# Five small changes to an attention and feed-forward kernel: fewer products of zeros, two copies moved to VectorE, a buffer swapped, a product put later, the last output split

## The chip, the cores and the metric

One core of a Trainium2 chip. The metric is the device time of the whole program in microseconds (us), median of several runs on the same chip. The spread of one kernel's runs is mostly 1 to 2 us of 924 (3.7 us once), and the changes here are of that size. So experiments were timed in five rounds on one chip beside the kernel before (three chips in all, so a kernel is compared with its own runs of the kernel before), and each also left one profile in which stages can be compared to 0.1 us.

## The reference

Attention in which a query sees only the keys of its own hash bucket, then a two-layer product with a PReLU between.

```python
def _attn_ref(q, k, v, proj):            # q, k, v: (4, 8, 768, 64), proj: (64, 6)
    q_bits = (np.einsum('bhsd,dk->bhsk', q, proj) > 0)   # k_bits likewise, then bucket numbers
    mask = q_bucket[:, :, :, None] == k_bucket[:, :, None, :]
    scores = np.where(mask, scale * np.matmul(q, k.transpose(0, 1, 3, 2)), -1e9)
    attn = np.exp(scores - max); attn = attn / (sum + 1e-09)
    return np.matmul(attn, v)
def _moe_ref(x, w_in, w_out, alpha):     # x: (3072, 512), d_ff 2048
    h = x @ w_in
    g = np.maximum(h, 0.0) + alpha * np.minimum(h, 0.0)
    return (g @ w_out)
```

## The kernel before

Attention runs in 32 units (16 pairs of heads, two halves of the queries). A unit has six key tiles. For each, TensorE writes scores into one of three score buffers of two banks, ScalarE takes the exp into SBUF, and VectorE and an accumulating transfer issued by GpSimd add up the six tiles. `attend` multiplies the exps with v into the only bank `av`; `totals` multiplies the sum with ones into the only bank `sm`; `divide` (VectorE) reads both. VectorE also prepares the weights meanwhile. The feed-forward blocks are called f_0 to f_7 and z_1 to z_7 in the profile, four times over; their weights come by transfers `wi` and `wl`. Other names in the profile: `sc` scores, `pt` exps, `accd` and `accp` the two partial sums of the key tiles (the accumulating transfer adds into `accp`, VectorE's last sum adds `accp` to `accd`), `x` the divided result. A transfer "lands" when its data have arrived.

```python
    def setup():
        ...
        ps = psum.tile([P, 512], F32, name="nil", tag="av")
        for i in range(12):
            do(PE.matmul(ps, zero[:, :P], zero, start=True, stop=True))
    def setup_alpha():
        ps = psum.tile([P, NF], F32, name="alps", tag="sm")
        do(PE.transpose(ps, alpha16, ident[:NF, :NF]))
        do(DVE.tensor_copy(alpha, ps))
    def two_banks(name):
        return psum.tile([P, 2, 512], F32, name=name, tag="sc", bufs=3)
    ...
    for u in range(UNITS):
        scores(u, 1)
        if u < last:
            scores(u + 1, 0)
        add_last(u); add_total(u)              # VectorE: sum of six key tiles
        ...                                    # next unit's first sum, hash, turns, weights
        attend(u, 0)                           # key tiles 0 to 2
        totals(u)                              # ones product
        ...                                    # weights
        attend(u, 1)                           # key tiles 3 to 5
        divide(u)
        ...
    for j, (b, what, n) in enumerate(blocks):  # feed-forward
        ...
            load_w(b * NI + n + 2)             # wi, two buffers
            if n >= NI - 2:
                load_w2(b, n - NI + 2)         # wl
```

`do` keeps an engine's instructions in program order. Transfers without it are placed on their queue by the framework.

## Time and profile before

| | |
|---|---|
| time | 924.33 us median of 3; medians of 924.2 to 924.7 in the later comparisons |
| first profile | span 923.9 us; that run took 925.64 us |
| TensorE busy | 907.8 us |
| TensorE gaps | head 6.25, attention from 250 us on about 2.6, tail 7.1 us |

"Span" is the profile's own length, some 1.8 us less than the time. The first profile came from a run 1.3 us above the median. One more piece: the chain of waits where attention ends (start, length, what ran).

```profile
359.58 0.97 DVE accd L721
360.55 0.04 issue
360.59 0.87 PE sm L743 x4
361.46 1.94 PE av L731 x12
363.39 1.49 PE f_0a L805 x4
```

VectorE's last sum ends at 360.54, then come the ones product and three key tiles of attend, and feed-forward goes on at 363.39.

### The profile page before, as it was taken

The page shows a single profiled execution, that of the slowest core. Times are in us where ns is not written, and L with a number is a line of the kernel's source. Part 1 is how long each engine was busy: PE and PEld are TensorE (multiplying, and loading weights), DVE is VectorE, ACT ScalarE, POOL GpSimd, SP SyncE. Part 2 cuts the span into 40 slices and gives each one's busy share as a digit, 9 for nine tenths or more (in the row PEclk, how much of TensorE's full clock was granted, in tenths as well). Part 3 has the DMA queues.
Part 4 walks back from the last instruction along what each step waited for, and adds up shares of the span by engine and source line. Part 5 has one row for each costly group of instructions (what it writes and reads, how often), then busy time and mean ns, then how long its engine had stood idle before and what let it go on. Part 6 is the DMA issues. An engine that isn't in the chain of part 4 may idle for free.

```text
span 923.9 us, 13627 instructions
## 1 busy us (share of the span) xinstructions
PE 907.8 (98%) x5073; PEld 605.4 (66%) x5073; DVE 754.0 (82%) x1316; ACT 422.6 (46%) x751; POOL 40.9 (4%) x50
## 2 busy tenths in 40 slices
PE   7999999999999999999999999999999999999996
PEld 4444444454444444556998556998556998556996
DVE  3899998999999998678987668978668978668985
ACT  7788888888877783222212222212222212222212
POOL 1111111111111110000000000000000000000000
PEclk9999999999999999999999999999999999999999
DMA  9576969798777844425333325334325333321232
GB/s 240 145 188 158 273 162 301 177 254 240 189 188 190 205 131 148 174 92 186 110 134 131 116 101 180 109 131 140 112 105 177 111 133 138 112 105 40 100 131 70
DMA packets 114059, 141.50 MB, mean 153 GB/s; under 512 B 54064, under 2 KB 102208, under 8 KB 110400
## 3 DMA queue, kind: packets, MB, share of 16 engines
q1 hardware_dynamic: 103680, 127.56, 43.4%
q0 software_dynamic: 8704, 12.58, 8.0%
q8 instruction: 42, 0.69, 0.3%
q10 hardware_dynamic: 1600, 0.39, 0.2%
q14 instruction: 33, 0.27, 0.1%
HBM read 100.67 MB, written 27.26 MB: 138 GB/s over the span
## 4 chain that ended last, share of the span: by engine, by line
PE 65%; DVE 16%; DMA 2%; issue 1%; ACT 0%; DVEq 0%; ACTq 0%
PE sc L698 3%; PE z_4a L805 2%; PE f_4a L805 2%; PE z_7a L805 2%; PE z_5a L805 2%; PE z_3a L805 2%; PE z_6a L805 2%; PE z_2a L805 2%; PE z_1a L805 2%; PE f_2a L805 2%; PE f_5a L805 2%; PE f_7a L805 2%; PE f_6a L805 2%; PE f_1a L805 2%; PE av L731 2%; PE f_0a L805 2%
## 5 line engine op out<-in xcount | busy, mean ns | idle before, releaser
L703 ACT ACTIVATE pt<-sc 128x768 f32<-128x768 f32 x192 | 153.1, 814 | 61.8 <-PE sc L698 60.1
L698 PE MATMUL sc<-qT,kT 64*128 64x384 f32 x768 | 155.1, 482 | 0.0
L731 PE MATMUL av<-pt,vn 128*64 128x385 f32 (+1 forms) x768 | 136.5, 491 | 0.0
L731 PEld LDWEIGHTS av<-pt,vn 128*64 128x64 f32 x768 | 52.3, 136 | 70.7 <-issue 63.8
L698 PEld LDWEIGHTS sc<-qT,kT 64*128 64x128 f32 x768 | 68.1, 188 | 34.8 <-issue 34.7
L855 DVE TENSOR_TENSOR g<-g,g 128x384 f32<-128x384 f32 x128 | 68.4, 555 | 2.2
L698 PE MATMUL sc<-qb,kb 64*128 64x384 bf16 x384 | 63.0, 324 | 2.8 <-ACT kb L684 2.2
L895 DVE TENSOR_TENSOR ws<-wl 128x512 f32<-128x512 f32 x56 | 38.5, 688 | 24.0 <-DMA wl<-w_out_s 24.0
L903 DVE TENSOR_TENSOR gs<-g,gs 128x768 f32<-128x768 f32 x56 | 53.5, 956 | 1.0
L903 DVE TENSOR_TENSOR gs<-g 128x768 f32<-128x768 f32 x56 | 53.4, 953 | 0.0
L713 POOL DMA_DIRECT2D accp<-pt x32 | 38.5, 1204 | 311.4 <-DVE accp L712 150.2
L851 DVE SCALAR_TENSOR_TENSOR g<-h,alpha 128x384 f32<-128x384 f32 x32 | 19.8, 618 | 36.0 <-ACT h L844 36.0
L698 PEld LDWEIGHTS <-kb 64*128 64x128 bf16 x384 | 19.2, 94 | 43.2 <-issue 19.9
L712 DVE TENSOR_TENSOR accp<-pt,pt 128x768 f32<-128x768 f32 x32 | 30.4, 951 | 10.0 <-ACT pt L703 10.0
L679 ACT ACTIVATE qb<-hs,hb 32x384 bf16<-32x384 f32 x64 | 36.7, 574 | 2.2 <-issue 1.1
L721 DVE TENSOR_TENSOR accd<-accd,accp 128x768 f32<-128x768 f32 x32 | 30.7, 958 | 5.1 <-DMA accp<-pt 4.1
L717 DVE TENSOR_TENSOR accd<-pt,pt 128x768 f32<-128x768 f32 x32 | 30.5, 952 | 3.6 <-ACT pt L703 3.6
L718 DVE TENSOR_TENSOR accd<-accd,pt 128x768 f32<-128x768 f32 x32 | 30.7, 959 | 3.3
L915 DVE TENSOR_TENSOR m<-m,m 128x768 f32<-128x768 f32 (+1 forms) x40 | 28.6, 716 | 1.9 <-ACT m L921 1.2
L743 PE MATMUL sm<-accd,ones 128*64 128x384 f32 x128 | 26.5, 492 | 3.2 <-DVE accd L721 3.1
L684 ACT ACTIVATE kb<-hs,hb 64x384 bf16<-64x384 f32 (+1 forms) x48 | 27.7, 578 | 0.6
L564 DVE TENSOR_SCALAR_CACHE_REDUCE wx<-wx 128x512 f32<-128x512 f32 x32 | 21.7, 679 | 2.9 <-ACT wx L558 2.9
(323 smaller groups left out, 1777.7 us busy)
## 6 DMA issues: line engine op xcount, KB each, us to landing
wi<-w_in_s SPq DMA_DIRECT2D x32, 896.0 KB, 4.6
wl<-w_out_s SPq DMA_DIRECT2D x28, 1024.0 KB, 4.8
accp<-pt POOLq DMA_DIRECT2D x32, 384.0 KB, 4.3
raw<-in_moe_w_in_dram SPq DMA_DIRECT2D x16, 512.0 KB, 4.0
raw<-in_moe_w_out_dram SPq DMA_DIRECT2D x16, 512.0 KB, 3.8
w_in_s<-wsi SPq DMA_DIRECT2D x16, 448.0 KB, 5.4
w_out_s<-wso SPq DMA_DIRECT2D x8, 896.0 KB, 5.5
vn<-in_v_dram SPq DMA_DIRECT2D x16, 384.0 KB, 4.5
```

The costliest lines, as they stand in the source:

```text
L679: do(ACT.activation(bits["q", pi][D * s : D * s + 32, cols], ps[c : c + 32, half, :CW], AF.Sign, bias=hb[c : c + 32],))
L698: do(PE.matmul(sc[:, s, :CW], what["k", pi][r, ks], what["q", pi][r, qs], start=first, stop=not first,))
L703: do(ACT.activation(pt[:, :, :CW], sc[:, :, :CW], AF.Exp, scale=SCALE / DOWN))
L713: nc.gpsimd.dma_start(accp[u], p(u, 2), accum_op=ALU.add)
L717: do(DVE.tensor_tensor(accd[u], p(u, 3), p(u, 4), op=ALU.add))
L718: do(DVE.tensor_tensor(accd[u], accd[u], p(u, 5), op=ALU.add))
L721: do(DVE.tensor_tensor(accd[u], accd[u], accp[u], op=ALU.add))
L731: do(PE.matmul(av[u][D * s : D * s + D, :w], nat["v", pi][:, s, kc * D : (kc + 1) * D], prob[u, kc][:, s, :w], start=(kc == 0), stop=(kc = ...
L805: do(PE.matmul(self.ps[bank], self.left(left, k), self.right(right, k), start=start and k == 0, stop=k == self.nk - 1, skip_group_check=no ...
L855: do(DVE.tensor_tensor(new_g(b, to)[:, i], g_m[b, x][:, i], g_m[b, y][:, i], op=ALU.subtract))
L895: do(DVE.tensor_tensor(t, w2[b, n, x], w2[b, n, y], op=op))
L903: do(DVE.tensor_tensor(t, g2[b, n, x], g2[b, n, y], op=ALU.subtract))
```

## The change

Each part aims at a gap of TensorE: (1) four products of zeros fewer before the first turn, (2) k's first two copies on VectorE, so that they run beside q's, (3) alpha's turn in a score buffer, not in the bank that the division holds, (4) the ones product behind five key tiles, to cover a late sum, (5) the last output turned in two goes, of which only the second waits for the last add.

```diff
-        for i in range(12):
+        for i in range(8):
             do(PE.matmul(ps, zero[:, :P], zero, start=True, stop=True))
@@
-        ps = psum.tile([P, NF], F32, name="alps", tag="sm")
+        ps = two_banks("alps")[:, 0, :NF]
@@ turn(), and its calls for pair 0
+        if engine is DVE:
+            do(DVE.tensor_copy(dst, ps[:, halves, :CW]))
+        else:
+            do(ACT.activation(dst, ps[:, halves, :CW], AF.Copy, ...))
...
+        turn(0, "q", half)
+        turn(0, "k", half, DVE)
@@
-        attend(u, 0)
+        attend(u, range(NC - 1))
         totals(u)
...
-        attend(u, 1)
+        attend(u, range(NC - 1, NC))
@@ every output now leaves in two transfers of 512-byte pieces
+        for i in range(2):
...
+                nc.sync.dma_start(dst[:, i, t0 : t0 + len(mine)], o[...])
@@
-    turn_out()
+    (end,) = to_turn
+    turn_part(*end, [(0, 0), (1, 0), (2, 0), (2, 1)])
+    turn_part(*end, [(0, 1), (1, 1)])
```

More of the change, by code (lines that the diff above doesn't have):

```diff
@@ L638, in fast_path, with turn @@
     BOTH = slice(0, 2)
-    def turn(pi, name, halves=BOTH):
+    def turn(pi, name, halves=BOTH, engine=None):
         src = nat[name, pi].rearrange("p c h d -> p c (h d)")
@@ L647, in turn @@
             do(PE.transpose(ps[:, c // CH, c % CH * P :][:, :P], src[:, c], ident))
-        do(ACT.activation(
-            tr[name, pi].rearrange("p (h w) -> p h w", h=2)[:, halves], ps[:, halves, :CW], AF.Copy,
-            scale=DOWN if name == "q" else 1.0,
-        ))
+        dst = tr[name, pi].rearrange("p (h w) -> p h w", h=2)[:, halves]
+        if engine is DVE:
+            do(DVE.tensor_copy(dst, ps[:, halves, :CW]))
+        else:
+            do(ACT.activation(dst, ps[:, halves, :CW], AF.Copy, scale=DOWN if name == "q" else 1.0))
     def magnitude(pi, name):
@@ L721, in add_total, with attend @@
         do(DVE.tensor_tensor(accd[u], accd[u], accp[u], op=ALU.add))
-    def attend(u, half):
+    def attend(u, kcs):
         pi, g = divmod(u, NCH)
-        if half == 0:
+        if kcs.start == 0:
             av[u] = psum.tile([P, 512], F32, name=f"av{u}", tag="av")
         w = CW + 1 if g == 0 else CW
-        for kc in range(half * NC // 2, (half + 1) * NC // 2):
+        for kc in kcs:
             for s in range(2):
@@ L734, in attend @@
                 ))
-        if half == 1 and g == 0:
+        if kcs.stop == NC and g == 0:
             vsum[pi] = pool.tile([P, 1], F32, name=f"vs{pi}", tag="vs")
@@ L939, in turn_out, with turn_part @@
         while to_turn:
-            b, p, half, ch = to_turn.pop(0)
-            ps = two_banks(f"to{b}_{p}")
-            flat = ps.rearrange("p a f -> p (a f)")
-            for t in range(CH):
-                for i in range(2):
-                    do(PE.transpose(flat[:, 2 * t * P + i * P :][:, :P], m2[b, p][:, i, t * P : (t + 1) * P], ident))
-            o = late[0].tile([P, CH, 2 * P], F32, name=f"o{b}_{p}", tag="o")
-            do(ACT.copy(o.rearrange("p t d -> p (t d)"), flat[:, : CH * 2 * P]))
-            nc.sync.dma_start(
-                out_v[b, ch * CH : (ch + 1) * CH].rearrange("c p d -> p c d")[:, :, half * 2 * P : (half + 1) * 2 * P], o,
-            )
+            turn_part(*to_turn.pop(0), [(t, i) for t in range(CH) for i in range(2)])
+    def turn_part(b, p, half, ch, parts):
+        ps = two_banks(f"to{b}_{p}")
+        flat = ps.rearrange("p a f -> p (a f)")
+        for n, (t, i) in enumerate(parts):
+            do(PE.transpose(flat[:, n * P : (n + 1) * P], m2[b, p][:, i, t * P : (t + 1) * P], ident))
+        o = late[0].tile([P, CH * 2 * P], F32, name=f"o{b}_{p}", tag="o")[:, : len(parts) * P]
+        do(ACT.copy(o, flat[:, : len(parts) * P]))
+        o = o.rearrange("p (n d) -> p n d", d=P)
+        dst = out_v[b, ch * CH : (ch + 1) * CH].rearrange("c p (h d) -> p h c d", d=P)[:, 2 * half : 2 * half + 2]
+        for i in range(2):
+            mine = [(n, t) for n, (t, ii) in enumerate(parts) if ii == i]
+            if mine:
+                n0, t0 = mine[0]
+                step = mine[1][0] - n0 if len(mine) > 1 else 1
+                nc.sync.dma_start(
+                    dst[:, i, t0 : t0 + len(mine)], o[:, n0 : n0 + step * (len(mine) - 1) + 1 : step],
+                )
     top = const.tile([P, 4], F32, name="top")
@@ L985, in fast_path @@
     load_part(0, "k", slice(CH, NC), nc.scalar)
-    for name in "qk":
-        turn(0, name, first)
-    hash_bits(0, first)
-    for name in "qk":
-        turn(0, name, second)
+    for half in (first, second):
+        turn(0, "q", half)
+        turn(0, "k", half, DVE)
+        if half is first:
+            hash_bits(0, first)
     load(1, "q")
```

## The prediction

> **What bounds the kernel now.** I read the page's engine shares first, then its forty slices, the sums by stretch, TensorE's own waits, and the timeline and the chain wherever TensorE has a gap.
>
> The page's busy times and slices:
> ```profile
> PE 907.8 (98%) x5073; PEld 605.4 (66%) x5073; DVE 754.0 (82%) x1316; ACT 422.6 (46%) x751; POOL 40.9 (4%) x50
> ...
> PE   7999999999999999999999999999999999999996
> ...
> DVE  3899998999999998678987668978668978668985
> ```
> TensorE (PE) is busy 907.8 of 923.9 us, so only 16.1 us can be had from its gaps. VectorE (DVE) is at nine tenths in the first 16 slices (attention, to 364 us) and lower after. Two engines are near their limit in attention; TensorE alone is in the feed-forward part.
>
> Sums by stretch (first figure after the stretch: its length, then PE busy, then PEld, DVE):
> ```profile
> 0.00:10.00 10.00, 7.00 (x38) 3.34 (x40) 0.87 (x12) 4.47 (x8) 2.35 (x18) 1.00 0.74 164
> 10.00:20.00 10.00, 8.35 (x64) 4.80 (x62) 4.75 (x9) 9.57 (x16) 1.33 (x1) 1.00 1.07 311
> 250.00:300.00 50.00, 48.65 (x346) 23.15 (x344) 47.77 (x85) 39.71 (x62) 6.00 (x5) 1.00 0.72 185
> 340.00:365.00 25.00, 23.86 (x137) 10.77 (x134) 23.12 (x46) 10.30 (x18) 2.41 (x2) 1.00 0.42 111
> 849.00:925.00 76.00, 67.78 (x418) 66.30 (x416) 57.91 (x93) 15.06 (x41) 0.00 (x0) 0.98 0.26 92
> ```
> The gaps lie in the head (6.25 us up to 40 us, with two stretches not shown), near the end of attention (1.35 + 0.1 + 1.14) and at the end (7.15 to 923.9). Between 365 and 849 us there is 0.14 us. The change can act only in the head, the attention's end and the tail. What it saves there carries to the end unchanged, because the part between is solid TensorE work.
>
> TensorE's waits:
> ```profile
> PE sm L743 <- DVE accd L721: 3.1, 6, 0.8
> PE nil L510 <- DVE wh L501: 1.2, 1, 1.2
> PE alps L523 <- DVE st L753: 1.0, 1, 1.0
> ```
> The first is the ones product (exp sums over partitions) waiting for VectorE's sum of six key tiles; the third is alpha's turn waiting for a bank.
>
> **What the Trainium skill says.**
> (1) "TensorE: Matmul & The Clock Gate", Part 1: the array starts at half clock, and about 3.4 us of sustained activity releases it, by time and not by number of products. The trace agrees: the products of zeros start at 1.19 us, come 0.43 us apart until 4.10 us and 0.216 us apart from there.
> (2) "VectorE: DVE Perf Modes", "Why PSUM operands drop a tier": an fp32 read from PSUM gets no speed-up, and its table gives (120 + elements)/0.96 GHz. For 384 elements that is 0.53 us, an estimate from that page. No such copy is in the trace; the 128x384 transpose out of PSUM takes 0.57 us.
> (3) "DMA: Bandwidth & Descriptors", "Anatomy of one DMA": about 2 us fixed plus a part by size. The output transfers here (384 KB) take 2.5 us to landing by the page.
> (4) "Perfetto Trace Analysis", "Identifying Performance Opportunities": repeated gaps on the saturated engine can mean that a buffer is missing. Alpha's 1.0 us is such a gap, but a single one.
>
> **Part 1, zero products, 12 to 8.** The four removed ones are the last, all at full clock.
> ```profile
> 3.73 0.15 PEld L510 LDWEIGHTS <-zero 128*128 128x128 bf16 x1 [0.28 <-issue]
> 4.10 0.75 PEld L510 LDWEIGHTS <-zero 128*128 128x128 bf16 x4 [0.22 <-issue]
> 4.97 0.46 PEld L647 LDWEIGHTS tp_q<-ident,qn 128*128 128x128 f32 x3
> ```
> 4 x 0.216 = 0.86 us. The first halves of q and k had landed by 3.8 and 4.03 us (semaphore events), ScalarE's table load ends at 4.43, so the turns can start at 4.32 instead of 5.18. The head follows 0.86 us earlier until something that does not move stops it.
>
> **Part 2, k's first copies on VectorE.** Now qT takes ScalarE 0.49 us from 5.71 and kT 0.48 from 6.10, ending 6.58. k's turn ends at about 6.00, so VectorE at 0.53 to 0.57 would end at 6.55 to 6.6: nothing gained. The second pair of copies is not on the path: the first exp waits for the scores, and they for kb. Worth 0 (+-0.1).
>
> **Part 3, alpha's turn.** It takes away the 1.02 us wait (39.70). But the rotation of three score buffers after the change is q's turn, k's turn, alpha, then the score tiles of unit 2: the third of them (key tile 5) gets alpha's buffer and must wait until VectorE has copied alpha. VectorE keeps its order, so this copy stays behind unit 1's division:
> ```profile
> 39.70 0.23 PE L523 MATMUL alps<-ident,alpha 16*128 16x16 f32 x1 [1.02 <-DVE st L753]
> ...
> 41.38 0.17 DVE L524 COPY alpha<-alps 128x16 f32<-128x16 f32 x1
> ...
> 41.49 0.33 PE L698 MATMUL sc<-qb,kb 64*128 64x384 bf16 x2
> ```
> The copy ends at 41.55; now key tile 5 starts at 41.49. From 23.79 to 41.55 VectorE is solid (gaps of 0.02 to 0.04 only), and that stretch began with a wait for a transfer:
> ```profile
> 23.79 0.96 DVE L721 TENSOR_TENSOR accd<-accd,accp 128x768 f32<-128x768 f32 x1 [2.02 <-DMA accp<-pt]
> ```
> So at unit 2 the gain of parts 1, 3 and of unit 0's ones product (0.86 + 1.02 + 0.58) collapses to what this landing moves. It is issued 0.86 earlier, but into queues that are full (DMA share 1.07 in 10:20), so I take 0.6. Gain at unit 2: 0.6 - (41.6 - 41.49) = **0.5 us**; the old wait of 1.02 becomes one of about 2 us at the scores of unit 2.
>
> **Part 4, ones product behind five key tiles.** It moves two key tiles of attend ahead of the ones product, 12 products in 1.94 us for three tiles, so 2 x 0.645 = 1.29 us of work to cover a late sum. From unit 3 to 21 TensorE sets the pace (10.43 and 11.08 us by turns, no gap). But VectorE falls behind at unit 12, where the chain shows
> ```profile
> 143.51 10.74 DMA accp<-pt
> ```
> against 4 us for nearly all other units, and from there to unit 31 it is solid: the ends of accd are 10.40 us apart, later 10.59, 11.46 while x is summed, and 10.60 up to 360.54. TensorE's waits for it (by the sums' ends against the end of the third key tile: 0.55, 0.32, 0.99, then 0.27, 0.92, 0.55, in all 3.6) therefore do not vanish: VectorE's last sum still ends at 360.54 less the 0.5. What is won is what TensorE need not do after it: one key tile instead of three, **1.29 us**. The feed-forward start has room: VectorE's division ends at 364.43 and its next operand at about 364.2.
>
> **Part 5, the last part in two goes.** Now:
> ```profile
> 916.41 0.32 ACT L921 COPY m<-z_4a 128x192 f32<-128x192 f32 x1 [1.66 <-PE z_4a L805]
> 916.76 0.36 DVE L915 TENSOR_TENSOR m<-m,m 128x192 f32<-128x192 f32 x1 [1.23 <-ACT m L921]
> 917.17 0.76 PE L945 MATMUL to<-ident,m 128*128 128x128 f32 x5 [0.69 <-DVE m L915]
> 917.97 0.80 ACT L947 COPY o<-to 128x768 f32<-128x768 f32 x1 [1.25 <-PE to L945]
> ```
> The last transfer is issued at 918.80 and its semaphore seen at 921.80, then 2.1 us of closing semaphores. Four of six turns do not need the last add. Afterwards: four turns 916.21 to 916.8; copy of 512 columns 916.85 to 917.44 (0.48 for 384, 0.80 for 768, so 0.59); two turns 917.17 to 917.55; copy of 256 columns (0.37) to 917.95. SyncE spends about 0.4 us on each issue and has two before it, so the last transfer goes out at 918.3, 0.5 earlier, with 128 KB in place of 384 and about 2.3 us (my estimate from 2.5 to 3.0 for 384 KB) instead of 3.0. Gain 0.5 + 0.7, less a little for sharing: **1.1 us**. All other outputs now take two issues and 512-byte pieces; they end well before the next w_out load (output at 459.95, load at 463.02), so they cost nothing.
>
> **Sum:** 0.5 + 1.3 + 1.1 = 2.9 us, 924.3 - 2.9 = **921.4 us**.
>
> **Rivals.** (a) The removed waits add up simply: 0.86 + 0.58 + 1.02 + 3.1 + 1.1 = 6.7 us, 917.7. Against it stand VectorE's solid stretches. It would need the late landing at unit 12 to go away; that transfer sits behind a burst of weight stores and loads whose place in the queue may change. Then up to 2 us more are won. (b) VectorE does not move at unit 2 and the alpha buffer's wait eats everything before it, or the late landing gets worse or comes to another unit of the solid stretch: 0.5 to 1.5 us less, 922.5. (c) With fewer zeros the clock falls back before the scores: a few products at half clock, under 1 us; for it speaks that the gap before the hash stays 0.6 us, against it that such gaps of up to 1.2 us cost no clock before. (d) Smaller output pieces delay w_out: TensorE would wait in feed-forward; its present slack of about 2 us speaks against it.
>
> **Range and chances.** Mostly the landings decide: 919.6 to 923.1. Two per cent would be 18.5 us, more than all gaps together: faster 0.01, same 0.98, slower 0.01.
>
> **What would show it.** Right: no wait of alps; a wait of 1.5 to 2.8 us of sc for alpha's copy; sm waits fewer but not gone; the first feed-forward product 1.5 to 2.1 us earlier; last issue about 0.5 us earlier relative to the last z product. Wrong: first scores not 0.86 us earlier, no wait at unit 2, VectorE with real gaps between units 13 and 31, a new slow accp landing.

## The result, and the profile after

The changed kernel takes **924.2 us** (median of 6, 923.27 to 926.98) against 924.26 (median of 6). The ratio is 1.0001, 95% interval 0.9988 to 1.0015. Ratios are the mean time of one kernel's fast runs over that of the other's of the same rounds, so not quite the ratio of the medians. The prediction was 921.4, with a range of 919.6 to 923.1: of the 2.9 us nothing shows. That the time would stay within 2% was right.

Busy times on the page of the changed kernel:

```profile
PE 906.2 (98%) x5069; PEld 605.7 (66%) x5069; DVE 755.0 (82%) x1318; ACT 421.5 (46%) x750; POOL 40.9 (4%) x50
```

TensorE's waits, changed kernel (us in total, times, longest):

```profile
PE av L732 <- DVE x L760: 2.4, 4, 0.9
...
PE f_2a L806 <- DMA wi<-w_in_s: 1.3, 1, 1.3
...
PE sc L699 <- DVE alpha L524: 0.4, 1, 0.4
PE sm L744 <- DVE accd L722: 0.3, 1, 0.3
```

The waits aimed at have gone: no line of `alps`, and 0.3 us in place of 3.1 for the ones product. But three waits have come in their place: attend for the `av` bank (which the division, `x`, releases), block 2 of feed-forward for its w_in, and scores for alpha's buffer. The chain where attention ends, changed kernel:

```profile
355.30 0.63 DVE x L760
355.93 0.04 issue
355.97 3.45 PE av L732 x20
359.42 0.65 PE sm L744 x4
360.06 0.65 PE av L732 x4
360.70 1.49 PE f_0a L806 x4
```

TensorE is now released by the division of unit 30, not by the sum of unit 31. The tail of the changed kernel, by the timeline:

```profile
914.87 0.32 ACT L922 COPY m<-z_4a 128x192 f32<-128x192 f32 x1 [1.66 <-PE z_4a L806]
915.22 0.36 DVE L916 TENSOR_TENSOR m<-m,m 128x192 f32<-128x192 f32 x1 [1.23 <-ACT m L922]
915.31 0.59 ACT L949 COPY o<-to 128x512 f32<-128x512 f32 x1
...
915.73 0.41 PE L947 MATMUL to<-ident,m 128*128 128x128 f32 x2 [0.46 <-DVE m L916]
916.22 0.37 ACT L949 COPY o<-to 128x256 f32<-128x256 f32 x1 [0.32 <-PE to L947]
```

The two goes work as designed: the last z product starts at 913.27 and the last copy ends at 916.59, 3.32 us later, against 918.77 - 914.80 = 3.97 before. Yet the span ends 9.18 us after the z product, before 9.06.

The two first profiles differ by 1.4 us in span while the medians of the times do not differ. So one profile each is not enough, and all later statements use milestones of all 14 profiles. In us from the span's start:

| kernel (profile) | zeros | full clock from | first scores | attend 11 ends | sum 12 ends | sum 31 ends | attend 31 ends | block 2 starts | last z starts | end |
|---|---|---|---|---|---|---|---|---|---|---|
| before, first | 12 | 4.04 | 9.47 | 147.49 | 155.30 | 360.54 | 363.39 | 377.62 | 914.80 | 923.86 |
| before, b_again | 12 | 5.62 | 10.24 | 146.35 | 154.26 | 359.50 | 362.36 | 376.58 | 913.35 | 922.43 |
| changed, first | 8 | 4.46 | 8.77 | 145.46 | 153.62 | 358.83 | 360.70 | 376.36 | 913.27 | 922.45 |
| changed, after_again | 8 | 6.42 | 9.49 | 145.99 | 154.47 | 359.61 | 361.48 | 375.87 | 912.68 | 922.30 |
| head | 8 | 13.76 | 10.44 | 148.20 | 155.73 | 360.97 | 363.82 | 378.05 | 914.99 | 924.03 |
| z8 | 8 | 7.07 | 9.67 | 146.59 | 154.87 | 360.10 | 362.95 | 377.18 | 914.87 | 924.11 |
| z4 | 4 | 14.12 | 9.47 | 147.90 | 156.05 | 361.28 | 364.14 | 378.36 | 915.14 | 924.18 |
| ones | 12 | 4.48 | 9.68 | 145.93 | 153.61 | 358.85 | 360.72 | 375.54 | 912.40 | 921.52 |
| after_z12 | 12 | 5.12 | 9.96 | 146.35 | 155.33 | 360.57 | 362.44 | 377.00 | 913.88 | 923.38 |
| tail | 12 | 6.04 | 10.45 | 146.57 | 154.34 | 359.57 | 362.42 | 376.65 | 913.41 | 922.59 |
| ones_wi | 12 | 4.12 | 9.50 | 145.99 | 151.92 | 357.72 | 359.59 | 373.82 | 925.67 | 935.81 |
| best3 | 12 | 4.87 | 9.88 | 146.13 | 151.82 | 357.82 | 359.69 | 373.91 | 910.64 | 919.81 |
| best4 | 12 | 4.93 | 9.91 | 146.30 | 151.99 | 365.19 | 367.06 | 381.28 | 918.53 | 927.57 |
| best5 | 12 | 7.11 | 10.93 | 147.17 | 152.86 | 358.92 | 360.80 | 375.02 | 911.80 | 920.69 |

"Full clock from" is when the throttle records grant TensorE its whole clock; "sum" is VectorE's sum of the six key tiles of that unit.

### The profile page after: what moved, and what is told of

Same layout as the page of the kernel before. It is cut to its first block, busy times and chain, and to the rows that moved or that the text cites. A ratio compares the mean times of both kernels' runs of the same rounds, so it can differ in the third digit from the quotient of the medians.

```text
span 922.4 us, 13645 instructions
## 1 busy us (share of the span) xinstructions
PE 906.2 (98%) x5069; PEld 605.7 (66%) x5069; DVE 755.0 (82%) x1318; ACT 421.5 (46%) x750; POOL 40.9 (4%) x50
## 4 chain that ended last, share of the span: by engine, by line
PE 82%; DVE 14%; DMA 2%; ACT 1%; issue 1%; DVEq 0%; ACTq 0%; POOLq 0%
PE sc L699 11%; PE av L732 8%; PE z_4a L806 2%; PE f_2a L806 2%; PE z_7a L806 2%; PE z_5a L806 2%; PE z_3a L806 2%; PE z_6a L806 2%; PE z_2a L806 2%; PE z_1a L806 2%; PE f_5a L806 2%; PE f_7a L806 2%; PE f_6a L806 2%; PE f_4a L806 2%; PE f_3a L806 2%; PE f_0a L806 2%
## 5 line engine op out<-in xcount | busy, mean ns | idle before, releaser
L806 PE MATMUL f_2a<-x,wi 128*128 128x384 f32 x64 | 23.4, 488 | 1.3 <-DMA wi<-w_in_s 1.3
```

The lines of the kernel that those rows point to most:

```text
L806: do(PE.matmul(self.ps[bank], self.left(left, k), self.right(right, k), start=start and k == 0, stop=k == self.nk - 1, skip_group_check=no ...
```

## The experiments

**The kernel before again (b_again).** No edit.

> The kernel before, unchanged, for a second profile and for the spread. Its first profile ran in 925.64 us, 1.3 over its median of 924.3. Transfer theory (gains are real up to the end of attention and then lost to a w_in load that limits the first feed-forward blocks): last product of unit 31's attend ends at 362.5 to 363.5 in the new profile too, and what differs from run to run lies behind it. Rival (the first profile was a slow sample of the head, so the gain of 2 us read there is no gain): it ends at 361.5 to 362.2, and unit 0's sum ends near 22.6 in place of 24.75. Time ratio 1.000 both.

924.3 us against 924.69, ratio 0.9999. Attention ends at 362.36, midway between the two expectations, and unit 0's sum at 23.52, nearer to the rival's. In this profile there is no wait of `alps` and none of 0.58 us at unit 0, both of which the prediction had counted as regular:

```profile
PE sm L743 <- DVE accd L721: 2.5, 5, 0.8
```

VectorE's last sum of unit 0, same profile (no bracket: no wait before it):

```profile
22.56 0.96 DVE L721 TENSOR_TENSOR accd<-accd,accp 128x768 f32<-128x768 f32 x1
```

The accumulating transfer of unit 0 was 2.02 us late in the first profile and not late here. The first profile was a slow sample of the head.

**Parts 1 to 3 alone (head).**

```diff
-        for i in range(12):
+        for i in range(8):
-        ps = psum.tile([P, NF], F32, name="alps", tag="sm")
+        ps = two_banks("alps")[:, 0, :NF]
+        turn(0, "k", half, DVE)      # and the copy in turn()
```

> Only parts 1 to 3 (8 products of zeros, k's first copies on VectorE, alpha in a score buffer). Transfer theory: first scores 0.7 us earlier, unit 2 about 2 us earlier than in the first profile of before, end of attention 1.7 earlier; time 0.3 to 1.7 us faster, with the w_in load of block 2 near its limit. Rival: first scores 0.7 us earlier, but unit 0's sum is set by the landing of its accumulating transfer, which does not follow: time within 0.4 us of before.

925.32 us against 924.69, ratio 1.0003 (0.9989 to 1.0016): no gain, and both theories were wrong about the first scores, which came at 10.44, later than before. The timeline of TensorE in this profile:

```profile
10.44 0.50 PE L699 MATMUL sc<-qb,kb 64*128 64x384 bf16 x2 [0.74 <-DVE kT L650]
10.71 1.51 PE L699 MATMUL sc<-qT,kT 64*128 64x384 f32 x4
```

and in the changed kernel's:

```profile
8.77 0.34 PE L699 MATMUL sc<-qb,kb 64*128 64x384 bf16 x2 [0.94 <-ACT kb L685]
8.95 0.81 PE L699 MATMUL sc<-qT,kT 64*128 64x384 f32 x4
```

The same instructions took 1.51 us in place of 0.81. TensorE ran at half clock until 13.76 us, with the same program head that had its full clock at 4.46 in the changed kernel's profile.

**Eight and four products of zeros alone (z8, z4).**

```diff
-        for i in range(12):
+        for i in range(8):        # z8; range(4) in z4
```

> Only the 8 products of zeros in place of 12. Clock theory (full clock comes by a window that does not start with the kernel; seen so far at 4.0, 5.6, 4.5 and 6.0 us with 12, at 4.5 and 13.8 us with 8): with 8 the array is sometimes not busy long enough for the window, so full clock comes either near 4 to 5 us or after 7 us; five runs spread by more than with 12 and their median is 0 to 1 us slower than before. Rival (my prediction: products at full clock are simply saved): full clock near 4.5 us, first scores at 8.6, 0.5 us or more faster.

> Only 4 products of zeros: a larger dose. The last ends near 2.9 us, but q and k land at 3.8 and 4.0 us. Clock theory: full clock after 7 us in nearly every run, first scores at half clock, 1 to 3 us slower than before. Rival: first turn at 4.1 us, earlier than with 8, at half clock for a short time only, time as before or up to 0.5 us faster.

z8: 924.11 us against 924.31, ratio 0.9999 (0.9985 to 1.0012), full clock from 7.07. z4: 926.03 against 924.31, ratio 1.0015 (1.0001 to 1.0029), full clock from 14.12, scores at 1.49 us as in head. Over all profiles full clock came between 4.04 and 7.11 us with 12 products, and at 4.46, 6.42, 7.07 and 13.76 with 8. With 8 the first scores come 0.4 us earlier on average (9.59 against 10.00 over all profiles), but that is lost again where the clock comes late: attend 11 ends at 146.56 on average with 8 and at 146.48 with 12. (Two of the four profiles with 8, head and z8, are of the slowest of their five runs.) For z8 neither the clock theory's loss nor the prediction's gain of 0.5 us was seen. The larger dose shows the direction: z4 is 1.7 us slower by the medians.

**Part 4 alone (ones).**

```diff
-        attend(u, 0)
+        attend(u, range(NC - 1))
         totals(u)
-        attend(u, 1)
+        attend(u, range(NC - 1, NC))
```

> Only part 4 (ones product behind five key tiles). Transfer theory: TensorE waits at the start of attend for the average's bank instead (2 to 3 us in all, near units 24 and 29 to 31), attention ends about 1.0 us earlier relative to VectorE's last sum, and a wait of up to 1.3 us for w_in in block 2 takes some back: 0.2 to 1.0 us faster. Rival (the whole of part 4 is taken back by the bank): end of attention at the same distance from VectorE's last sum as before, 2.8 us, time within 0.3 us.

923.82 us against 924.69, ratio 0.999 (0.9977 to 1.0004); by the interval not clear of zero. From sum 31 to the end of attend it is 1.87 or 1.88 us in all eight profiles with part 4, and 2.85 or 2.86 in all six without: part 4 gains 0.98 us there. From the end of attend to block 2 it is 14.22 or 14.23 us in all six profiles without part 4. With part 4 and the old order of loads it is 15.66, 14.39, 14.82 and 14.56: 1.43, 0.17, 0.60 and 0.34 us are given back while block 2 waits for w_in. The waits of this run:

```profile
PE av L731 <- DVE x L759: 2.2, 4, 0.9
...
PE f_2a L805 <- DMA wi<-w_in_s: 0.4, 1, 0.4
```

**Part 5 alone (tail).** The edit is the last two pieces of the diff above.

> Only part 5 (outputs in two transfers, last part in two goes). From start of the last z product to the end of the span: 9.1 us before. My prediction: 8.0. Reading of the changed kernel's profile: the last issue comes 0.35 earlier but 768 pieces of 512 bytes in place of 384 of 1024 land 3.1 us after it, and the closing wait chain takes up the rest: 9.0 to 9.2 and a time within 0.3 us of before. If smaller output pieces delay w_out loads, waits of z products for them appear and it is slower by over 0.5.

924.72 us against 924.69, ratio 1.0002. From the last z product to the end: 9.18 us. No z product waits for w_out, so the smaller pieces cost nothing there. In this profile the three issues lie 2.65, 3.06 and 3.65 us after the z product's start (one at 4.00 before); the 768 pieces of 512 bytes land from 3.55 to 6.35 (384 of 1024 bytes from 4.89 to 6.57 in b_again); and SyncE's closing chain has one wait more, 0.37 us at 8.02.

**The changed kernel with 12 products of zeros (after_z12).**

```diff
-        for i in range(8):
+        for i in range(12):
```

> The changed kernel with 12 products of zeros again (part 1 undone). Clock theory: full clock by 6.1 us at the latest, and 0.3 to 1 us faster than before, as the run of part 4 alone (923.8 against 924.7). Rival (part 1 gains, something else in the change loses): 0.5 us or more slower than the changed kernel's 924.2.

924.84 us against 924.31, ratio 1.0006 (0.9992 to 1.002). The expected gain did not come. The table shows where it went in this profile: unit 12's sum came 8.98 us after attend 11 (7.5 to 8.5 in the others with the old order of loads), and the tail took 9.50. So restoring part 1 does not rescue the change, and neither side's sign is settled by the time.

**Part 4 with the order of loads kept (ones_wi).**

```diff
-            nc.sync.dma_start(w_m[n], w_in_s[n % NI])
+            do(nc.sync.dma_start(w_m[n], w_in_s[n % NI]))
-            nc.sync.dma_start(t, w_out_s[SIDES[ORDER[n]][0]])
+            do(nc.sync.dma_start(t, w_out_s[SIDES[ORDER[n]][0]]))
```

> Part 4 alone, with the loads of w_in and of w_out's products kept in program order on their queue, so that w_out's first two loads (2 MB) go after block 2's w_in and the first two w_in loads leave the stretch where unit 12's accumulating transfer is late. Transfer theory: no wait of block 2 for w_in (0.43 and 1.27 us in the two profiles with part 4), unit 12's sum no longer 3 us late, end of attention up to 2 us earlier than in part 4 alone, 1 to 3 us faster than before. Rival (these waits are hidden by VectorE's own load): the same time as part 4 alone, 0.9 us faster than before.

937.92 us, ratio 1.015: a miss in time, a hit in mechanism. Unit 12's sum comes 5.93 us after attend 11, block 2 starts 14.23 us after attention. But w_out's first loads of each batch now come too late:

```profile
PE z_1a L805 <- DMA wl<-w_out_s: 5.5, 3, 2.0
...
PE z_2a L805 <- DMA wl<-w_out_s: 1.6, 2, 1.0
```

and right after one such gap, of 1.98 us, TensorE lost its full clock for 3.4 us (from 574.1): eight products took 2.74 us there, and 1.57 after a gap of 1.92 us at 717.7, which cost no clock.

**The changed kernel again (after_again).** No edit.

> The changed kernel, unchanged, for a second profile and five more times. Sum theory: from VectorE's sum of unit 12 to that of unit 31 it is 205.2 us, as in all nine profiles without a changed order of loads; attention ends 1.87 us after that sum (2.85 before); the start of the second product of feed-forward then gives back 0.4 to 1.5 us at block 2's w_in; from the last z product to the end 9.2 to 9.5 (9.05 before). Time within 0.6 us of before. Rival (the changed kernel is 0.5 to 1 us faster and the chip's spread hid it): 923.5 or less, ratio interval below 1.

924.08 us against 924.2, ratio 0.9994 (0.998 to 1.0008). Milestones as the sum theory expects, except that block 2 gave back only 0.17 us, and the tail took 9.62 us, more than expected.

**Only the loads that matter (best3).** Part 4; the first three `wi` loads in program order; w_out's first two loads directly behind the third, in batch 0 only.

```diff
+            dma = nc.sync.dma_start(w_m[n], w_in_s[n % NI])
+            if n <= 2:
+                do(dma)
@@ the feed-forward loop
+            if j == 0:
+                load_w2(b, 0)        # both with do() in batch 0
+                load_w2(b, 1)
+            elif b and n >= NI - 2:
+                load_w2(b, n - NI + 2)
```

> Part 4 alone, with the first three w_in loads kept in program order and w_out's first two loads put right behind the third. Transfer theory: unit 12's sum comes 5.9 us after unit 11's attend in place of 7.5 to 9.0, block 2 does not wait, attention's gain of 0.98 is kept, and no z product waits for w_out: 2 to 3 us faster than before (921.3 to 922.4). Rival: another unit's accumulating transfer or another load takes the burst and the time stays at that of part 4 alone, about 1 us faster.

**921.68 us against 924.2**, ratio 0.9979 (0.9965 to 0.9992). Unit 12's sum comes 5.69 us after attend 11, attention's 0.98 is kept (1.87), block 2 starts 14.22 after it, and nothing waits for w_out. The wait for the sums has gone; that for the `av` bank is left:

```profile
PE av L731 <- DVE x L759: 1.6, 3, 0.9
```

Unit 12 in the kernel before (first profile), where the first two w_in loads are issued 1.0 us before the accumulating transfer (at 143.51):

```profile
142.49 1.12 SPq L784 DMA_DIRECT2D wi<-w_in_s  x2
...
154.34 0.96 DVE L721 TENSOR_TENSOR accd<-accd,accp 128x768 f32<-128x768 f32 x1 [2.04 <-DMA accp<-pt]
```

and in best3, where they are issued only at 222.46 and 224.69:

```profile
150.86 0.96 DVE L721 TENSOR_TENSOR accd<-accd,accp 128x768 f32<-128x768 f32 x1
```

This settles both transfers as causes (they were moved together, but each is read at its own stage): with them out of the way part 4's gain reaches the end, and unit 12 gives about 2 us more, of which 0.8 is lost again on the way to unit 31 (206.00 us from sum to sum). By the medians best3 beats the kernel before and, at 924.08 in the same rounds, the changed one by 2.4 to 2.5 us; by the ratio it gains 1.9 us on the kernel before (0.7 to 3.2).

**Also VectorE's sums of x on GpSimd (best4).**

```diff
-            sum_x(0, u - HW - 4, DVE)
+            sum_x(0, u - HW - 4, POOL)
```

> The same, and the four sums of x (units 20 to 23, 0.95 us each on VectorE) on GpSimd. VectorE-bound theory: the 205.2 us from unit 12's to unit 31's sum shrink by up to 3.8 us, down to about 202 where TensorE's own work is the bound; TensorE's waits at units 22 to 24 vanish; 1.5 to 3.5 us faster than with VectorE's sums (919 to 920.5). Rival (GpSimd's sums slow VectorE on the shared memory port, or hold up the accumulating transfers that GpSimd issues): 205 or more, no gain or a loss.

929.45 us, ratio 1.0056: slower. A VectorE instruction that takes 0.44 us in best3 takes 3.13 beside GpSimd's sum:

```profile
240.49 3.13 DVE L568 TENSOR_SCALAR wr<-wx 128x512 uint32<-128x512 uint32 x1
```

```profile
241.03 2.30 POOL L778 TENSOR_TENSOR x<-x,x 128x768 f32<-128x768 f32 x1
```

The Trainium skill, "SBUF — State Buffer", section "Who interferes with whom", says that the two share a port pair, and that GpSimd and a VectorE instruction in a mode that uses both its ports block each other: whoever issues first holds the pair for the whole instruction. The trace agrees in kind: beside each of GpSimd's four sums (2.26 to 2.30 us) one TENSOR_SCALAR of VectorE takes 2.77 to 3.23 us in place of 0.43 or 0.44. The mode and who came first cannot be read (VectorE's starts 0.54 us earlier in the lines, but spans on GpSimd are rough). VectorE loses 10.2 us in these four, and 3.8 us of sums are taken off it; from sum 12 to sum 31 it takes 213.20 us, 7.2 more than in best3. The other half of the rival is small: the sums wait 0.5 us in all for accumulating transfers. This also confirms VectorE as what bounds that stretch: what VectorE loses, attention loses. TensorE lost its full clock here too, for 3.4 us from 288.2, after a wait of 2.43 us; 20 products of attend took 5.15 us there, and 3.45 after a longer wait of 2.71 us at 262.3. So the length of a gap alone did not decide it.

**best3 with the last part in two goes and one transfer (best5).**

```diff
+    for i in range(2):               # half i turned and copied on its own, i = 0 needs no last add
+        ...
+        do(ACT.copy(o[:, :, i * P : (i + 1) * P], flat.rearrange("p (t d) -> p t d", d=P)))
+    nc.sync.dma_start(..., o)        # one transfer, 1 KB pieces
```

> best3 with the last part turned and copied in two goes (first the half that needs no last add, then the other), but sent as before in one transfer of 1 KB pieces, and all other outputs as before. Transfer theory (part 5 gains nothing because its three transfers of 512-byte pieces land no earlier and lengthen the closing chain): the copy ends about 0.55 us earlier after the last z product than before (3.97), the one issue is at about 3.45 in place of 4.00, and the span ends 8.4 to 8.6 after the z product in place of 9.05 to 9.2; time about 0.5 us under best3, 921.2. Rival (TensorE's closing branch, at 6.5 to 6.8, or another part of the closing chain bounds the end whatever is sent): 9.0 or more.

922.2 us against 924.31, ratio 0.9977 (0.9964 to 0.9989): the same as best3 within the noise. The issue came at 3.35 us after the z product, 0.65 earlier, as expected. But the pieces land from 4.24 to 6.39, against 4.89 to 6.66 in best3: only 0.27 us earlier at the end, and the span ends at 8.89 instead of 9.17 (9.10 is the average with the old last part). So both expectations failed: it is not only the 512-byte pieces, and the end is not fixed either.

## Why the prediction was wrong

**Reading the bound: right, but from one sample.** TensorE and VectorE are near their limits in attention, TensorE alone after it. But the step "What it saves there carries to the end unchanged, because the part between is solid TensorE work" failed. TensorE was solid at block 2 because its w_in had landed shortly before it was needed: needed about 6.26 us after its issue, it landed after 4.5 to 5.3 us in the six profiles without part 4. It is issued 7.96 or 7.97 us after the end of attend in every profile, so with part 4 it went out earlier too. But the 2 MB of w_out ahead of it on the queue go out 5.9 us after sum 31 with part 4 or without, as their loads wait for the last store of VectorE's weights; w_in now followed them after 3.56 us in place of 4.55, landed only after 6.4 to 7.6 us, and 0.17 to 1.43 us were lost. Shown by best3, where w_in goes ahead of w_out: it lands after 4.7 us, and the loss is gone.

**Part 1, 0.86 us: the failing step is "the turns can start at 4.32 instead of 5.18".** It took the clock's coming at 4.10 us as part of the program. It is not: 4.04 to 7.11 us with 12 products in nine profiles, though the first product starts at 1.19 or 1.20 in all, so 2.8 to 5.9 us of products where the prediction quotes about 3.4. The page cited for the clock, "TensorE: Matmul & The Clock Gate", Part 1, says in the same place that the window is free-running and that the moment varies from run to run; the prediction used only the first half of it. The traces agree: in every profile the full clock is held for a multiple of 3.413 us (269 times that in the first profile, 266 in head), and both times that it was lost it was for one such step, while the moment of its coming differs from run to run. Of the four profiles with 8 products only one had its first scores near the 8.6 us that follow from this step (8.77; the others 9.49, 9.67, 10.44). The products removed run at full clock only in some runs, and with fewer products the clock can come much later (13.76 in head, 14.12 in z4). The rival (c) of the prediction named this and sized it "under 1 us"; head's profile shows scores at half clock until 13.76. On average parts 1 to 3 are worth 0, as far as four profiles with a spread of 2.7 us can tell: attend 11 ends at 146.56 with 8 products and 146.48 with 12; with the old order of loads sum 12 ends at 154.67 and 154.57.

**Part 2, 0: right.** k's copy takes VectorE 0.56 us (0.53 to 0.57 predicted), and the hash still waits 0.65 us for it, 0.63 before. That k's second copy is off the path held in the changed kernel but not in head, at half clock: there the first scores waited for it, until 10.44.

**Part 3: mechanism right, size wrong.** The new wait for alpha's buffer came, but as 0.38 and 0.19 us in the changed kernel's two profiles, where about 2 us was predicted. In two more profiles with the new place (head, after_z12) there was none. And there was usually no wait of 1.02 us to remove: of ten profiles with the old place two had one (1.02, 0.75), the other eight 0.3 us or less. It went with unit 0's late transfer (2.02 us late in the profile with 1.02, 0.93 in that with 0.75). That lateness, on which the 0.5 us rested, was not regular: 0.55 us or less in the other 12 profiles.

**Part 4, 1.29 us: right in kind, 0.98 in size, and then given back.** VectorE does set the pace from unit 12 on: from sum 12 to sum 31 it is 205.14 to 205.24 us in all ten profiles with the old order of loads, with part 4 and without. The waits for the sum did not simply shrink. TensorE ran ahead until it met the only `av` bank, held until the division of the unit before. That costs 0.31 of the 1.29. After block 2 (0.63 on average over the four profiles) and 0.10 more from block 2 to block 3 (9.13 us in the four profiles with part 4 and the old order of loads, 9.03 in all others), 0.25 us are left.

**Part 5, 1.1 us: the failing step is "with 128 KB in place of 384 and about 2.3 us".** (Its 2.5 us for 384 KB is the median on the profile's page.) The issue came 0.35 earlier (0.5 predicted), but the last piece landed no earlier (6.31 to 6.83 us after the z product, 6.55 on average; 6.53 to 6.66 and 6.58 with one transfer in the eight profiles named below), and in all four profiles the closing chain has a further wait of 0.37 to 0.45 us. The four profiles with part 5 take 9.18, 9.62, 9.50 and 9.18 us from the last z product to the end, 9.37 on average; the eight with the old last part, without the disturbed ones_wi (10.14), take 9.04 to 9.24, 9.10 on average. Part 5 loses 0.27 on average. What holds the last pieces stays open, but the packet records narrow it. A 16 KB packet of an instruction queue takes 1.01 to 1.46 us there, and in all four profiles with part 5 the last piece ends 0.84 to 0.89 us after that packet's end, so the end follows it one for one. The packet starts at 4.46 to 4.49, against 3.97 to 4.13 with the old last part. The last dozen pieces come 22 to 24 ns apart, as from a single DMA engine. This fits a packet that sits on the engine which finishes last; the records do not name the engine, so it is not shown.

**The sum** is therefore 0 (head) + 0.25 (part 4) - 0.27 (part 5) = 0 us, in place of 0.5 + 1.3 + 1.1. Measured: 0.06 and 0.12 us faster by the medians of the two comparisons, with intervals some 2.5 us wide that contain 0. Two slips in the prediction's sums change nothing in this: the tail's gap was 7.08 us, not 7.15, and rival (a) counts unit 0's 0.58 us twice, as the 3.1 has it already.

One sign of being right was met by luck: "the first feed-forward product 1.5 to 2.1 us earlier". It starts at 360.70 and 361.48 in the changed kernel's two profiles, at 363.39 and 362.36 before, 1.8 us earlier on average; but sum 31 accounts for 0.8 of this, and over all profiles the stages up to sum 31 show no such gain.

**The rivals.** (a), the late landing at unit 12 going away, is real and worth over 1 us by unit 31, but the change did not touch it; best3 did. (b), that landing getting worse, was seen in part: in the three profiles of the changed kernel, with 8 or 12 products, sum 12 ends 8.16, 8.48 and 8.98 us after attend 11, in the seven others with the old order of loads 7.53 to 8.28; why is open. (d), w_out delayed by smaller pieces, did not happen. What no rival had was that the w_in load of block 2, hidden until now, becomes the bound as soon as the work before it gets shorter.

## What to carry to other kernels

Before booking a saved wait, look at the next transfer that the earlier TensorE will meet, and at its margin: a load that lands just in time shows no wait, and takes the gain. Take two or three profiles before sizing gaps of a microsecond, because the time at which the clock rises and the landing of a transfer in a crowded queue differ from run to run of one kernel. Here the order of a few loads was worth 1.0 us by the ratios and 1.6 by the medians (best3 against part 4 alone, each against its own runs of before), more than all five changes together.

## What the Trainium skill lacked or had wrong

- "TensorE: Matmul & The Clock Gate", Part 1, puts the rise of the clock around 4 us into sustained products, give or take 0.5 us. Here it came 2.8 to 5.9 us after the first of 12 products (nine profiles) and 3.3 to 12.6 us after the first of 8 (four). The page gives no figure for a warm-up that ends too early: scores at 1.51 us in place of 0.81 until 13.76.
- The same page has no figure for a gap as short as those that cost the clock here: 1.98 us (ones_wi) and 2.43 us (best4), while 1.92 and 2.71 us in the same runs did not.
- "VectorE: DVE Perf Modes", section "The TRN2 errata", gives 0.53 us (an estimate by its formula) for an fp32 copy of 384 columns out of PSUM; the trace has 0.56.
- No page gives a figure for how far an instruction packet can hold up the last output, or how much of an earlier issue reaches its landing. Here the last piece ended 0.84 to 0.89 us after a 16 KB instruction packet in all four profiles with part 5; the end moved by 0.27 us when the issue moved by 0.65 (best5), and by 0.2 at most when two thirds were sent ahead (tail).
